# Pooled attention and a tanh MLP in one kernel: w2 in another order, its sums spread over two groups, leftover scores in one visit

## The chip, the cores and the metric

The kernel runs on one core of a Trainium2 chip. The metric is the device time of one execution in microseconds: the median over runs. The engines named below are TensorE (PE in the profile, with its weight loads as PEld), VectorE (DVE), ScalarE (ACT), GpSimd (POOL) and SyncE (SP, which here only issues transfers). They run their own instruction lists in order and wait for each other by semaphores.

## The reference

For each of 8 batches and 8 heads, q, k and v are 576 tokens by 64. k and v are averaged over runs of 8 tokens, which leaves 72 pooled tokens; every token of q attends to them. The heads are then laid side by side, which gives 4608 tokens by 512, and an MLP follows whose activation is h - tanh(h):

```python
k_p = k.reshape(B, H, Sp, pool, D).mean(axis=3)      # Sp = 576 / 8 = 72
v_p = v.reshape(B, H, Sp, pool, D).mean(axis=3)
scores = scale * np.matmul(q, k_p.transpose(0, 1, 3, 2))
attn = softmax(scores)
x = np.matmul(attn, v_p).transpose(0, 2, 1, 3).reshape(B * S, H * D)
h = x @ w_in                                         # 512 -> 2048
out = (h - np.tanh(h)) @ w_out                       # 2048 -> 512
```

Inputs and output are float32; the kernel computes the matmuls in 16-bit types and sums in float32.

## The kernel before

**Groups and batches.** The MLP works on 9 groups of 512 tokens. Group g (0 to 7) is the first 512 tokens of batch g, and group 8 gathers the last 64 tokens of all batches (`xT_last`). While TensorE works on the MLP of group g, the attention of batch g + 1 is mixed in between, one visit at a time. All instruction order is written out by hand (`tc.manual_schedule()`): the order of the calls in the source is the order on each engine.

**The MLP of groups 1 to 8.** `h_pair` makes two of the 16 hidden tiles (8 matmuls on `w1b`, line 534), ACT takes the tanh of both (line 546) and DVE subtracts (`Gt`, line 547). With `NP` = 8, pairs 0 to 6 are followed by pair 7 in two halves (`h_one`, lines 551 and 552). The second product isn't made as one 2048 by 512 matmul but in seven products of half the rows and half the columns (`products`, line 614), which are combined by a few additions. They need sums of blocks of w2, held in `w2s`, and sums of hidden tiles (`P`, `Q`, `Dg`, lines 555 to 570). With w2 as 16 tiles of 128 rows, b11 and b12 are the left and right columns of tiles 0 to 7, b21 and b22 those of tiles 8 to 15. `w2s[0]` is b11 + b22, `[1]` b11 + b12, `[2]` b21 + b22, `[3]` b21 - b11 and `[4]` -b22; b12 itself is replaced by b22 - b12. The seven products use, in order, `w2s[3]`, b11, `w2s[4]`, b12, `w2s[0]`, `w2s[1]`, `w2s[2]`, each in two halves of four tiles, so there are 14 steps u. `w_sum` (line 573) makes a sum, over a part k0 to k1 of the eight tiles.

**Group 0** runs while weights are still coming. It uses the plain product: `mlp_o` (line 517) adds four w2 tiles to one of four token blocks, in 16 steps u: `qd` = u // 4 is the set of four w2 tiles, `tb` = u % 4 the token block. Around these steps stand the attention of batch 1 and the sums of w2 that group 1 needs. w2 comes in four transfers of 512 KB (`load_w2`), issued by POOL: the first two early, the last two (`mid`) between the first and second step of pooling k of batch 1 (`pool_k(1)`, lines 256, 263, 266). SP's load of k of batch 2 is made to wait for the third w2 transfer (`after(load_k(2), w2_dmas[2])`). In the steps of group 0:

- u = 3: TensorE turns the pooled k of batch 1 (`kd`, line 320), DVE copies it to `KB`; from here also the turns of q (line 225), copied by ACT.
- u = 4: DVE makes all of `w2s[1]`, then pools v; POOL then makes `w2s[3]` in four parts, held back until v is pooled.
- u = 4 to 8: the scores of batch 1, tile by tile.
- u = 9 and 11: ACT makes `w2s[4]`.
- u = 9 to 13: `av` makes x for token blocks 0 to 3 and, as block 4, the last 64 tokens; `x_pe_transpose` (line 467) turns blocks 0 to 3, and ACT copies them to `xT` (line 474). The fourth turn stands ahead of step 14.
- u = 12 to 15: the finished token blocks are copied out of PSUM, by ACT for tb 0 and 2 and by DVE for tb 1 and 3 (line 526).

The rest of the sums is made on DVE: b12 after group 0, `w2s[0]` in four parts behind pairs 0 to 3 of group 1, and `w2s[2]` in two halves after products 1 and 2 of group 1.

**Scores.** 144 pooled tokens of two heads don't fit in 128 rows, so four tiles hold 128 rows each and the four leftovers of 16 rows are packed as tile `NM` = 4: four matmuls with 32 columns of weights each, which write four strips of one PSUM bank. `scores_wide(b, (t,))` makes 512 tokens of one tile and its Exp (line 374); `scores_tail(b)` makes the last 64 tokens of all five tiles, tiles 0 to 3 first, and their Exp (line 380). In groups 1 to 6, step u = 4 of the products is followed by the leftover tile's 512 tokens and step u = 5 by the tail.

**After the products.** DVE's `gate` instruction (line 635, after product 2) releases POOL's pooling of k and v of the batch after next. ACT's copy (line 644) and DVE's subtraction (line 645) follow product 4. `x_dma_transpose` (line 452) has SP transpose x for the next group.

Of the kernel before, what the change touches and what calls it, by code (L numbers as in the profile page):

```python
# [8 lines left out]
FP32 = mybir.dt.float32  # L9
BF16 = mybir.dt.bfloat16  # L10
F16 = mybir.dt.float16
ACT = mybir.ActivationFunctionType
ALU = mybir.AluOpType
PSUM = bass.MemoryType.PSUM

B, H, S, D = 8, 8, 576, 64
# [5 lines left out]
QA = 128 * R  # L22
QT = S - QA
# [6 lines left out]
NT = 5  # L30
# [2 lines left out]
LO = PR - 128  # L33
KP = 160
NM = 4
HT = TG // 2
HD = DM // 2
NP = NHID // 2
# [4 lines left out]
def kernel(  # L43
# [202 lines left out]
    def halves(n, b):  # L246
        return ((0, n),) if b < 2 else ((0, n // 2), (n // 2, n))

    def pool_k(b, eng, t0=0, t1=NT, mid=(), dep=None):
        r = k_raw[b % 2].rearrange("p t (j d) -> p t j d", d=D)[:, t0:t1, :, :]  # L250
        if b not in kdups:
            kdups[b] = work.tile([128, NT, 2, D], BF16, name="kd", tag="kd")
        kd = kdups[b][:, t0:t1, :, :]
        n = t1 - t0
        for ta, tb in halves(n, b):
            first = eng.tensor_tensor(  # L256
                out=r[:, ta:tb, 0:4, :], in0=r[:, ta:tb, 0:4, :], in1=r[:, ta:tb, 4:8, :], op=ALU.add
            )
            if dep is not None and ta == 0:
                after([first], dep)  # L260
        for c in mid:
            load_w2(c)
        eng.tensor_tensor(
            out=r[:, :, 0:2, :], in0=r[:, :, 0:2, :], in1=r[:, :, 2:4, :], op=ALU.add
        )
        eng.tensor_tensor(
            out=kd,
            in0=r[:, :, 0:1, :].to_broadcast([128, n, 2, D]),
            in1=r[:, :, 1:2, :].to_broadcast([128, n, 2, D]),
            op=ALU.add,  # L270
        )
        return first

    def pool_v(b, eng):
        r = v_raw[b % 2].rearrange("p t (j d) -> p t j d", d=D)
# [100 lines left out]
    def scores_tail(b):  # L376
        ps = ps_any([128, NT, QT], FP32, "s_ps")
        for t in range(NT):
            score_mms(b, t, ps[:, t, :], True)
        nc.scalar.activation(  # L380
            out=E_tiles[b][:, :, QA:S], in_=ps[:, :, :], func=ACT.Exp, scale=SCALE
        )

    def av_mms(b, blk, half, ps):
        E = E_tiles[b]
# [77 lines left out]
    def x_pe_transpose(b, blk, x_sb):  # L463
        xf = x_sb.rearrange("p a h d -> p (a h d)")
        ps = ps_any([128, NFB, 128], FP32, "xT_ps")
        for fb in range(NFB):
            nc.tensor.matmul(
                ps[:, fb, :],
                lhsT=xf[:, fb * 128 : (fb + 1) * 128],
                rhs=ident[:, :],  # L470
                start=True,
                stop=True,
            )
        nc.scalar.copy(out=xT[b % 2][:, blk, :, :], in_=ps[:, :, :])
# [33 lines left out]

    o_tiles = {}

    def mlp_o(g, tb, i0, i1, gts, pool=None):
        if i0 == 0:
            p, tag = pool or (ps_o, "o_ps")
            o_tiles[tb] = p.tile([128, DM], FP32, name="o_ps", tag=tag)
        o_ps = o_tiles[tb]
        for i in range(i0, i1):
            nc.tensor.matmul(  # L517
                o_ps[:, :],
                lhsT=gts[i][:, tb * 128 : (tb + 1) * 128],
                rhs=w2b[:, i, :],  # L520
                start=(i == 0),
                stop=(i == NHID - 1),
            )
        if i1 == NHID:
            o_sb = O[:, tb, :]
            (nc.vector.tensor_copy if g == 0 and tb % 2 else nc.scalar.copy)(
                out=o_sb, in_=o_ps[:, :]
            )
            nc.sync.dma_start(out=out_part(g, tb, tb + 1), in_=O[:, tb : tb + 1, :])

    def h_mms(g, i, dst):
# [40 lines left out]
    def w_sum(out, a, b, op, eng=nc.vector, k0=0, k1=NP):  # L572
        return eng.tensor_tensor(  # L573
            out=out[:, k0:k1, :], in0=a[:, k0:k1, :], in1=b[:, k0:k1, :], op=op
        )
# [90 lines left out]
        )  # L666

    def load_w2(c):
        w2_dmas.append(
            nc.gpsimd.dma_start(  # L670
                out=w2b[:, c * 4 : (c + 1) * 4, :], in_=w2_src[:, c * 4 : (c + 1) * 4, :]
            )
        )

    def after(lds, dep):
# [205 lines left out]
    for i in range(5, NHID):  # L881
# [5 lines left out]
        if i == 11:  # L887
            av(0, 4, ps_any, False)
            x_dma_transpose(0, 2)
    pool_k(1, nc.gpsimd, mid=(2, 3))  # L890
    after(load_k(2), w2_dmas[2])
    load_v(2)
    o_pools = [(ps_o, "o_ps"), (ps_o, "o_ps"), (ps_h, "hT_ps"), (ps_h, "hT_ps")]
    pend = []
    for u in range(16):
        qd, tb = u // 4, u % 4
        if u == 14:
            x_pe_transpose(1, *pend.pop(0))
        mlp_o(0, tb, qd * 4, qd * 4 + 4, gts, o_pools[tb])
        if u == 0:  # L900
            q_cast(1, nc.scalar.copy, 2)
            load_q(2)
        if u == 3:
            k_transpose(1, ps_any, (nc.vector.tensor_copy, nc.vector.tensor_copy))
            q_pe_transpose(1, (0,), "act")
        if u == 4:
            q_pe_transpose(1, (1,), "act")
            w_sum(w2s[:, 1, :, :], b11, b12, ALU.add)
            v1_done = pool_v(1, nc.vector)
            after(  # L910
                [
                    w_sum(w2s[:, 3, :, :], b21, b11, ALU.subtract, nc.gpsimd, k, k + 2)
                    for k in range(0, NP, 2)
                ],
                v1_done,
            )
        if u in (5, 6):
            q_pe_transpose(1, (u - 3,), "act")
        if 4 <= u <= 8:
            scores_wide(1, (u - 4,))  # L920
        if u == 6:
            q_pe_tail(1)
        if u == 8:
            scores_tail(1)
        if u in (9, 11):
            n = (u - 9) // 2
            nc.scalar.mul(
                out=w2s[:, 4, 4 * n : 4 * n + 4, :], in_=b22[:, 4 * n : 4 * n + 4, :], mul=-1.0
            )
        if u >= 9:  # L930
            if 11 <= u <= 13:
                x_pe_transpose(1, *pend.pop(0))
            if u <= 13:
                x_sb = av(1, u - 9, ps_any, False)
                if u < 13:
                    pend.append((u - 9, x_sb))
    pool_k(2, nc.gpsimd)
    pool_v(2, nc.gpsimd)
    w_sum(b12, b22, b12, ALU.subtract)
# [1 line left out]
    for g in range(1, NG):  # L941
        nb = g + 1 if g + 1 < B else None
        nn = g + 2 if g + 2 < B else None
        for p in range(NP - 1):
            c = p if g > 1 else p - 1
            if nb is not None and 0 <= c < 3:
                q_cast_part(nb, c)
            h_pair(g, p, ((2, 0, 4, 6, 0, 2, 4) if g == 1 else (0, 2, 4, 6, 0, 2, 4))[p], p % 2)
            if g == 1 and p < 4:
                w_sum(w2s[:, 0, :, :], b11, b22, ALU.add, k0=2 * p, k1=2 * p + 2)  # L950
            if 3 <= p < 6:
                sum_p(2 * p - 6, 2 * p - 4)
            if nb is not None and p == 0:
                k_dma_transpose(nb)
            if g == 1 and p == 0:
                x_dma_transpose(1, 2)
            if g > 1 and p == 0:
                store(g - 1, 2, 4, nc.gpsimd)
                store(g - 1, 0, 2, nc.gpsimd)
            if nb is not None and p == 0:  # L960
                k_place(nb, nc.gpsimd.tensor_copy)
            if nb is not None and 0 <= c < 3:
                q_dma_transpose(nb, c)
            if nb is not None and c == 2:
                if nn is not None:
                    load_k(nn)
                    load_v(nn)
                    load_q(nn)
        h_one(g, NP - 1, 1, 0, 2)
        h_one(g, NP - 1, 0, 1, 3)  # L970
        sum_p(6, 8)
        sum_q(0, 4)
        sum_q(4, 8)
        ps_a = Banks(2, 3, 4, 5, 0, 1)
        for u in range(14):
            n, half = u // 2, u % 2
            bk, lhs, rhs = products[n]
            if n == 6 and g == NG - 1:
                break
            product(g, bk, lhs, rhs, 4 * half, 4 * half + 4, n < 2)  # L980
            if half:
                after_product(g, n)
                if g == 1 and n in (1, 2):
                    w_sum(w2s[:, 2, :, :], b21, b22, ALU.add, k0=4 * n - 4, k1=4 * n)
            if nb is not None:
                if u < NT:
                    scores_wide(nb, (u,))
                if u == NT:
                    scores_tail(nb)
                if u in (5, 6, 7, 8, 10):  # L990
                    blk = (5, 6, 7, 8, 10).index(u)
                    av(nb, blk, ps_b1, True)
                    if blk in (1, 3, 4):
                        x_dma_transpose(nb, blk // 2)
                if u == 6 and nn is not None:
                    pool_k(nn, nc.gpsimd, dep=gate[0])
                    pool_v(nn, nc.gpsimd)
        if g < NG - 1:
            nc.scalar.copy(out=O[:, 0:2, 0:HD], in_=chain(g, C1))
# [37 lines left out]
```

## Time and profile before

| | us |
|---|---|
| median of 3 runs | 291.96 (291.9 to 292.7) |
| the profiled execution | 292.5 |
| its span | 290.8 |
| granted TensorE clock (mean) | 0.998 |
| TensorE busy | 280.6 |
| DVE busy | 220.1 |
| ACT busy | 151.1 |
| POOL busy | 118.7 |

The span is what the profile's rows cover; all times of rows are counted from its start. A row of a timeline has its start, its duration, the engine, the line of the source, the operation, what it writes and reads, how many instructions it joins, and in brackets how long the engine was idle before it and what ended that. Matmuls overlap: a 128x512 one lasts 0.379 in the rows, but the next starts 0.216 later, so for TensorE the distance between starts counts. `128*32` is the shape of the weights: 128 rows, 32 columns. The chain of waits is the list of work that ended last, followed back from the end.

### The profile page before, as it was taken

The page shows a single profiled execution, that of the slowest core. Times are in us where ns is not written, and L with a number is a line of the kernel's source. Part 1 is how long each engine was busy: PE and PEld are TensorE (multiplying, and loading weights), DVE is VectorE, ACT ScalarE, POOL GpSimd, SP SyncE. Part 2 cuts the span into 40 slices and gives each one's busy share as a digit, 9 for nine tenths or more (in the row PEclk, how much of TensorE's full clock was granted, in tenths as well). Part 3 has the DMA queues.
Part 4 walks back from the last instruction along what each step waited for, and adds up shares of the span by engine and source line. Part 5 has one row for each costly group of instructions (what it writes and reads, how often), then busy time and mean ns, then how long its engine had stood idle before and what let it go on. Part 6 is the DMA issues. An engine that isn't in the chain of part 4 may idle for free.

```text
span 290.8 us, 5231 instructions
## 1 busy us (share of the span) xinstructions
PE 280.6 (96%) x2031; PEld 177.7 (61%) x2032; DVE 220.1 (76%) x349; ACT 151.1 (52%) x216; POOL 118.7 (41%) x128
## 2 busy tenths in 40 slices
PE   7899989998999999999999999999999999999994
PEld 3454445544874589447944795479547954884583
DVE  6558757799984998499839993999389938945983
ACT  4737476585527660866086608661766146315510
POOL 8600726993099109910992089208930010010000
PEclk9999999999999999999999999999999999999999
DMA  7999999998745994599458956895560340012014
GB/s 249 225 213 277 301 156 299 322 199 299 190 80 108 303 315 91 111 283 344 82 108 262 352 97 106 252 352 108 100 163 0 62 166 2 1 52 95 0 36 111
DMA packets 64104, 49.95 MB, mean 172 GB/s; under 512 B 39248, under 2 KB 53072, under 8 KB 64080
## 3 DMA queue, kind: packets, MB, share of 16 engines
q1 hardware_dynamic: 54592, 35.60, 46.8%
q0 software_dynamic: 6768, 12.06, 19.0%
q10 hardware_dynamic: 2720, 1.97, 2.4%
q8 instruction: 16, 0.26, 0.4%
q14 instruction: 8, 0.07, 0.1%
HBM read 36.70 MB, written 9.44 MB: 159 GB/s over the span
## 4 chain that ended last, share of the span: by engine, by line
PE 75%; DMA 9%; DVE 6%; POOL 4%; ACT 2%; issue 1%; SPq 0%; POOLq 0%; DVEq 0%; ACTq 0%
PE PS L534 34%; PE PS L590 30%; DMA w1b<-in_moe_w_in_dram 5%; DMA k_raw<-in_k_dram 4%; PE PS L391 4%; PE PS L517 4%; PE PS L359 3%; DVE Gt L547 2%; DMA xT<-x_sb 1%; POOL k_raw L256 1%; DVE w2s L573 1%; DVE P L555 1%; ACT TS L546 1%; DVE x_sb L424 1%; ACT q_bf L193 1%
## 5 line engine op out<-in xcount | busy, mean ns | idle before, releaser
L534 PE MATMUL PS<-xT,w1b 128*128 128x512 bf16 x448 | 98.0, 379 | 1.2 <-DMA xT<-x_sb 0.7
L547 DVE TENSOR_TENSOR Gt<-PS,TS 128x1024 bf16<-128x1024 f32 x56 | 68.3, 1220 | 37.6 <-ACT TS L546 37.6
L534 PEld LDWEIGHTS <-w1b 128*128 128x128 f16 x512 | 49.9, 98 | 60.6 <-issue 1.9
L546 ACT ACTIVATE TS<-PS 128x1024 f32<-128x1024 f32 x56 | 57.3, 1024 | 31.6 <-PE PS L534 27.4
L256 POOL TENSOR_TENSOR k_raw<-k_raw 128x512 f32<-128x512 f32 (+2 forms) x13 | 21.1, 1639 | 83.3 <-DVE rden L423 53.8
L590 PE MATMUL PS<-w2s,Dg 128*128 128x256 f16 x256 | 30.2, 273 | 0.0
L374 ACT ACTIVATE E<-PS 128x512 bf16<-128x512 f32 x40 | 23.7, 598 | 12.0 <-PE PS L359 11.9
L590 PEld LDWEIGHTS <-P 128*128 128x128 bf16 x256 | 24.5, 98 | 6.1 <-issue 1.4
L590 PEld LDWEIGHTS <-Gt 128*128 128x128 bf16 x256 | 24.2, 98 | 6.1 <-DVE Gt L552 0.5
L606 POOL DMA_DIRECT2D out_dram<-O x14 | 7.8, 557 | 46.4 <-DVE O L647 44.2
L590 PEld LDWEIGHTS <-Dg 128*128 128x128 bf16 x256 | 24.8, 98 | 2.8
L555 DVE TENSOR_TENSOR P<-Gt 128x1024 bf16<-128x1024 bf16 x32 | 22.4, 699 | 0.5
L644 ACT COPY m<-PS 128x512 f32<-128x512 f32 x8 | 4.7, 585 | 31.8 <-PE PS L590 31.8
L391 PE MATMUL PS<-VB,E 128*128 128x130 bf16 x240 | 20.2, 220 | 0.1
L565 DVE TENSOR_TENSOR Dg<-Gt 128x1024 bf16<-128x1024 bf16 x32 | 19.9, 683 | 0.0
L277 POOL TENSOR_TENSOR v_raw<-v_raw 128x512 f32<-128x512 f32 (+1 forms) x12 | 19.4, 1640 | 0.0
L391 PEld LDWEIGHTS <-E 128*128 128x128 bf16 x240 | 16.3, 98 | 2.0 <-issue 0.4
L424 DVE TENSOR_TENSOR x_sb<-PS,rden 128x512 bf16<-128x512 f32 x24 | 16.6, 691 | 0.8
L590 PE MATMUL PS<-w2s,Gt 128*128 128x256 f16 x128 | 16.7, 273 | 0.4 <-DVE Gt L552 0.2
L590 PE MATMUL PS<-w2s,P 128*128 128x256 f16 x128 | 16.3, 273 | 0.0
L590 PE MATMUL PS<-w2s,Q 128*128 128x256 f16 x128 | 16.3, 273 | 0.0
L590 PE MATMUL PS<-w2b,P 128*128 128x256 f16 x128 | 16.3, 273 | 0.0
(114 smaller groups left out, 388.0 us busy)
## 6 DMA issues: line engine op xcount, KB each, us to landing
k_raw<-in_k_dram SPq DMA_DIRECT2D x7, 1024.0 KB, 7.7
q_raw<-in_q_dram SPq DMA_DIRECT2D x7, 1024.0 KB, 12.4
v_raw<-in_v_dram SPq DMA_DIRECT2D x7, 1024.0 KB, 11.4
out_dram<-O POOLq DMA_DIRECT2D x14, 512.0 KB, 4.6
w1b<-in_moe_w_in_dram POOLq DMA_DIRECT2D x4, 512.0 KB, 14.5
w2b<-in_moe_w_out_dram POOLq DMA_DIRECT2D x4, 512.0 KB, 18.6
out_dram<-O SPq DMA_DIRECT2D x4, 256.0 KB, 5.6
k_raw<-in_k_dram SPq DMA_DIRECT2D x7, 128.0 KB, 8.3
```

The source lines that it names most:

```text
L256: first = eng.tensor_tensor(out=r[:, ta:tb, 0:4, :], in0=r[:, ta:tb, 0:4, :], in1=r[:, ta:tb, 4:8, :], op=ALU.add)
L277: eng.tensor_tensor(out=r[:, ta:tb, 0:4, :], in0=r[:, ta:tb, 0:4, :], in1=r[:, ta:tb, 4:8, :], op=ALU.add)
L374: nc.scalar.activation(out=E[:, t, 0:QA], in_=ps[:, :], func=ACT.Exp, scale=SCALE)
L391: nc.tensor.matmul(ps[:, 2 * n : 2 * n + 2, :].rearrange("p h d -> p (h d)") if n < 2 else ps.rearrange("p (a s) d -> p a s d", s=2)[:, :, ...
L424: nc.vector.tensor_tensor(out=x_sb[:, :, :, :], in0=ps[:, :, :, 0:D], in1=rden[:, :, :, :].to_broadcast([128, 2, 4, D]), op=ALU.mult,)
L517: nc.tensor.matmul(o_ps[:, :], lhsT=gts[i][:, tb * 128 : (tb + 1) * 128], rhs=w2b[:, i, :], start=(i == 0), stop=(i == NHID - 1),)
L534: nc.tensor.matmul(dst, lhsT=w1b[:, fb, i * 128 : (i + 1) * 128], rhs=x[:, :, fb, :], start=(fb == 0), stop=(fb == NFB - 1),)
L546: nc.scalar.activation(out=t2, in_=PS[:, b0 : b0 + 2, :], func=ACT.Tanh)
L547: nc.vector.tensor_sub(out=Gt[:, p, :, :], in0=PS[:, b0 : b0 + 2, :], in1=t2)
L555: nc.vector.tensor_tensor(out=P[:, a:b, :], in0=Gt[:, a:b, 0, :], in1=Gt[:, a:b, 1, :], op=ALU.add)
L565: return nc.vector.tensor_tensor(out=Dg[:, a:b, :, :], in0=Gt[:, a:b, :, 0:HT], in1=Gt[:, a:b, :, HT:TG], op=ALU.subtract,)
L590: nc.tensor.matmul(part(g, bk, tt), lhsT=lhs(k, slice(tt * 128, (tt + 1) * 128)), rhs=rhs[:, k, :], start=(first and k == 0 and (tt == 0 o ...
```

## The change

- The four transfers of w2 bring tiles 0 to 3, 8 to 11, 4 to 7 and 12 to 15 (`W2_ORDER`), and group 0 uses them in this order.
- The last step of pooling k of batch 1 (`kd`) is made by DVE instead of POOL. POOL's first two parts of `w2s[3]` (tiles 0 to 3) follow that step; its other two still wait until v is pooled.
- At u = 4, DVE makes the first halves (k 0 to 3) of `w2s[1]`, `w2s[0]` and `w2s[2]` ahead of pooling v, and the second half of `w2s[1]` behind it. In group 1 only the second halves of `w2s[0]` (two parts, behind pairs 0 and 1) and of `w2s[2]` (after product 4, behind line 645) are left.
- `scores_ends` replaces the leftover tile's visit and the tail's visit, in group 0 at u = 8 and in groups 1 to 6 at u = 4: the leftover tile's 512 tokens, its 64 tail tokens, the tail of tiles 0 to 3, and then both Exp.
- In group 0, `av` of batch 1's last tokens comes after step 15, and the fourth turn of x after step 14 instead of ahead of it.
- All four token blocks of group 0 are copied out by ACT.

```diff
+W2_ORDER = (0, 8, 4, 12)
-    def pool_k(b, eng, t0=0, t1=NT, mid=(), dep=None):
+    def pool_k(b, eng, t0=0, t1=NT, mid=(), dep=None, last=None):
...
-        eng.tensor_tensor(
+        kd_done = (last or eng).tensor_tensor(
             out=kd,
...
-        return first
+        return kd_done
...
+    def scores_ends(b):
+        E = E_tiles[b]
+        ps = ps_any([128, QA], FP32, "s_ps")
+        pt = ps_any([128, NT, QT], FP32, "s_ps")
+        score_mms(b, NM, ps[:, :], False)
+        for t in (NM, 0, 1, 2, 3):
+            score_mms(b, t, pt[:, t, :], True)
+        nc.scalar.activation(out=E[:, NM, 0:QA], in_=ps[:, :], func=ACT.Exp, scale=SCALE)
+        nc.scalar.activation(out=E[:, :, QA:S], in_=pt[:, :, :], func=ACT.Exp, scale=SCALE)
...
-    def mlp_o(g, tb, i0, i1, gts, pool=None):
-        if i0 == 0:
+    def mlp_o(g, tb, qd, gts, pool=None):
+        if qd == 0:
...
-        for i in range(i0, i1):
+        i0 = W2_ORDER[qd]
+        for i in range(i0, i0 + 4):
...
-        if i1 == NHID:
-            o_sb = O[:, tb, :]
-            (nc.vector.tensor_copy if g == 0 and tb % 2 else nc.scalar.copy)(
-                out=o_sb, in_=o_ps[:, :]
-            )
+        if qd == 3:
+            nc.scalar.copy(out=O[:, tb, :], in_=o_ps[:, :])
...
     def load_w2(c):
+        i = W2_ORDER[c]
...
-                out=w2b[:, c * 4 : (c + 1) * 4, :], in_=w2_src[:, c * 4 : (c + 1) * 4, :]
-            )
+            nc.gpsimd.dma_start(out=w2b[:, i : i + 4, :], in_=w2_src[:, i : i + 4, :])
...
-    pool_k(1, nc.gpsimd, mid=(2, 3))
+    kd1 = pool_k(1, nc.gpsimd, mid=(2, 3), last=nc.vector)
+    after([w_sum(w2s[:, 3, :, :], b21, b11, ALU.subtract, nc.gpsimd, k, k + 2) for k in (0, 2)], kd1)
...
     for u in range(16):
         qd, tb = u // 4, u % 4
-        if u == 14:
-            x_pe_transpose(1, *pend.pop(0))
-        mlp_o(0, tb, qd * 4, qd * 4 + 4, gts, o_pools[tb])
+        mlp_o(0, tb, qd, gts, o_pools[tb])
...
         if u == 4:
             q_pe_transpose(1, (1,), "act")
-            w_sum(w2s[:, 1, :, :], b11, b12, ALU.add)
+            w_sum(w2s[:, 1, :, :], b11, b12, ALU.add, k1=4)
+            w_sum(w2s[:, 0, :, :], b11, b22, ALU.add, k1=4)
+            w_sum(w2s[:, 2, :, :], b21, b22, ALU.add, k1=4)
             v1_done = pool_v(1, nc.vector)
             after(
                 [
                     w_sum(w2s[:, 3, :, :], b21, b11, ALU.subtract, nc.gpsimd, k, k + 2)
-                    for k in range(0, NP, 2)
+                    for k in (4, 6)
                 ],
                 v1_done,
             )
+            w_sum(w2s[:, 1, :, :], b11, b12, ALU.add, k0=4)
...
-        if 4 <= u <= 8:
+        if 4 <= u <= 7:
             scores_wide(1, (u - 4,))
...
         if u == 8:
-            scores_tail(1)
+            scores_ends(1)
...
-        if u >= 9:
-            if 11 <= u <= 13:
-                x_pe_transpose(1, *pend.pop(0))
-            if u <= 13:
-                x_sb = av(1, u - 9, ps_any, False)
-                if u < 13:
-                    pend.append((u - 9, x_sb))
+        if 11 <= u <= 14:
+            x_pe_transpose(1, *pend.pop(0))
+        if 9 <= u <= 12:
+            pend.append((u - 9, av(1, u - 9, ps_any, False)))
+        if u == 15:
+            av(1, 4, ps_any, False)
...
-            if g == 1 and p < 4:
-                w_sum(w2s[:, 0, :, :], b11, b22, ALU.add, k0=2 * p, k1=2 * p + 2)
+            if g == 1 and p < 2:
+                w_sum(w2s[:, 0, :, :], b11, b22, ALU.add, k0=2 * p + 4, k1=2 * p + 6)
...
-                if g == 1 and n in (1, 2):
-                    w_sum(w2s[:, 2, :, :], b21, b22, ALU.add, k0=4 * n - 4, k1=4 * n)
+                if g == 1 and n == 4:
+                    w_sum(w2s[:, 2, :, :], b21, b22, ALU.add, k0=4)
             if nb is not None:
-                if u < NT:
+                if u < NM:
                     scores_wide(nb, (u,))
-                if u == NT:
-                    scores_tail(nb)
+                if u == NM:
+                    scores_ends(nb)
```

More of the change, by code (lines that the diff above doesn't have):

```diff
@@ L668, in load_w2 @@
     def load_w2(c):
+        i = W2_ORDER[c]
         w2_dmas.append(
-            nc.gpsimd.dma_start(
-                out=w2b[:, c * 4 : (c + 1) * 4, :], in_=w2_src[:, c * 4 : (c + 1) * 4, :]
-            )
+            nc.gpsimd.dma_start(out=w2b[:, i : i + 4, :], in_=w2_src[:, i : i + 4, :])
         )
```

## The prediction

> **What bounds the kernel now.** I read the page, then the granted clock, then the busy time by stretch, the chain of waits, and last the timelines of the engines in the stretches that the change touches.
>
> ```profile
> span 290.8 us, 5231 instructions
> PE 280.6 (96%) x2031; PEld 177.7 (61%) x2032; DVE 220.1 (76%) x349; ACT 151.1 (52%) x216; POOL 118.7 (41%) x128
> ```
>
> By stretch (length, then busy time of PE, PEld, DVE, ACT, POOL, the granted clock and DMA):
>
> ```profile
> 55.24:69.71 14.47, 13.98 (x66) 6.27 (x65) 13.53 (x15) 9.33 (x10) 12.07 (x11) 1.00 0.97 243
> 69.71:86.90 17.19, 16.13 (x159) 13.16 (x158) 16.17 (x28) 6.70 (x13) 7.10 (x5) 1.00 0.66 172
> 116.51:146.02 29.51, 29.51 (x223) 19.61 (x223) 23.02 (x34) 16.09 (x22) 15.50 (x16) 1.00 0.76 202
> ```
>
> TensorE bounds it, at a granted clock of 1.00. Group 3 (116.51 to 146.02) is 29.51 us of TensorE without a gap; group 1 (55.24 to 86.90) takes 31.66, and in it DVE is busy 29.70 of 31.66. So the question is group 1's DVE, and what TensorE does in the other groups. The chain of waits shows where DVE leads:
>
> ```profile
> 63.65 1.14 DVE Gt L547
> 64.79 0.98 DVE w2s L573
> 65.77 1.02 DVE P L555
> ...
> 71.52 0.61 DVE Gt L552
> 72.17 0.39 PE PS L590 x2
> ...
> 83.72 3.04 DMA xT<-x_sb
> ```
>
> From 63.65 DVE never rests until the last half of Gt; the first product's last two matmuls start only at 72.17, and the next group waits for the transposed x until 86.90 (0.67 idle). TensorE's own timeline around the moved parts:
>
> ```profile
> 38.56 0.45 PE L320 MATMUL PS<-ident,kd 128*128 128x128 bf16 x5 [0.86 <-POOL kd L266]
> 44.35 1.02 PE L517 MATMUL PS<-w2b,Gt 128*128 128x512 f16 x4
> 53.29 0.38 PE L467 MATMUL PS<-ident,x_sb 128*128 128x128 bf16 x4 [0.32 <-ACT xT L474]
> 135.55 0.40 PE L359 MATMUL PS<-qT,KB 128*32 128x512 bf16 x4
> 135.88 1.05 PE L590 MATMUL PS<-w2s,P 128*128 128x256 f16 x8
> 136.77 0.42 PE L359 MATMUL PS<-qt,KB 128*128 128x64 bf16 x8
> 137.12 0.52 PE L391 MATMUL PS<-VB,E 128*128 128x130 bf16 x6
> ```
>
> The numbers to take are the distances between starts.
>
> **kd of batch 1 on DVE: 0.** POOL's last step (1.54) goes; DVE does it in 0.82, the 128x640 f32 add at 43.56. TensorE would start the turn at 37.85, not 38.56. But the first score then waits for ACT's copy of qT: ACT casts q without a gap from 37.07 (its DMA) to 39.5 and ends that copy at 40.06, so the score starts at 40.1 instead of 40.20. And at 44.35 the third set of w2 tiles in the output product waits for the third w2 transfer: TensorE was free at 44.22, and SP's load of k, held by the same transfer, issues at 44.32. Its place among POOL's issues (33.80) is the same. So of 0.7 nothing remains; bounds 0 and 0.1. The three half sums put ahead of v's pooling on DVE (3 x 0.60 from about 39.3, blocked by POOL's two sums until 40.3 at worst) end by 42.1; v's transfer lets pooling start at 42.03. The fourth (0.69 behind it, done 46.7) precedes the first reciprocal, which comes at 47.0. POOL's other two sums now wait for the last w2 transfer (ACT waited for it until 47.95) and end at 50.25; POOL's next work waits for k until 51.00 in either kernel.
>
> **Leftover scores in one visit: 0.20 a visit, seven visits.** In group 3 the product ahead of the narrow (128*32) matmuls takes 0.97 to them (134.58 to 135.55), elsewhere 0.87: 0.10 in. Out of them 0.33 for a stream that costs 0.22 at full width: 0.11 out. The tail's four full and four narrow ones take 0.35; a stream of 64 columns is an eighth of 0.22, 0.03, and if the narrow four run side by side as the wide four do, that is 5 x 0.03, so here too 0.2 is going in and out. The new order (NM wide, NM tail, then 0 to 3) goes in and out once: 0.20 saved. No row shows a narrow matmul behind another on the same strip; if it drained in between, 0 is saved, and if strip after strip drained, it costs 0.1 x 3 = 0.3 extra. I take 0.20, the row nearest by being the same instructions. The tail's Exp (0.44) now stands ahead of ACT's copy L634: E ends 136.6, the Exp 136.95, and the product that L634 waits for now ends 137.1, so DVE's chain behind it, up to the x that the next group waits for, is at most 0.1 later. The transposed x lands 0.4 to 0.7 ahead of its use in groups 3 to 6 (in group 4 issued at 171.7, 3.1 to land, used at 175.46) and about 0.3 in group 2, which covers this and the 0.20. The Trainium skill, "TensorEngine Tiling (Array Packing)", Key Properties, says that a change of tiling mode, and not of the tile alone, drains the engine; by it 0.20 stands and both bad ends fall, and no run here shows it yet.
>
> **Batch 1's last tokens behind group 0: 0.55.** At 53.29 the fourth x turn sits in the bank of the third, 0.48 after av's last matmul could have handed over; in the new order the turn takes a bank read long before, and av (0.35) fills the end while ACT copies the last xT (done 54.3). The third av loses its 0.07 delay too. All four O copies are ACT's: the last ends at 54.9, its bank is wanted at 56.2, and the first Tanh comes at 56.4. With 0.20 for the visit, group 1 starts at 54.5 instead of 55.24: -0.75. The last tokens' reciprocals end at 55.6 and then the b12 sum starts; before it waited for the O copy until 56.05.
>
> **Group 1, first part.** The tanh chain moves by 0.75, so Gt of pair 3 starts at 62.9. The sum at 64.79 (0.98 on the chain) is gone. From there 8.4 us remained to 72.05; now 7.4, ending at 70.3 (-1.75). But DVE and POOL hold each other up, as rows of the two engines' timelines show:
>
> ```profile
> 64.45 1.05 POOL L291 TENSOR_TENSOR VB<-v_raw,mask 128x512 bf16<-128x512 f32 x1
> 64.70 1.07 DVE L573 TENSOR_TENSOR w2s<-w2b 128x512 f16<-128x512 f16 x1
> ...
> 79.64 3.04 POOL L256 TENSOR_TENSOR k_raw<-k_raw 128x512 f32<-128x512 f32 x2 [11.96 <-DVE m L635]
> 82.76 1.54 POOL L263 TENSOR_TENSOR k_raw<-k_raw 128x640 f32<-128x640 f32 x1
> 83.61 1.23 DVE L645 TENSOR_TENSOR m<-m,m 128x512 f32<-128x512 f32 x1
> 84.37 1.87 POOL L266 TENSOR_TENSOR kd<-k_raw 128x640 bf16<-128x640 f32 x1
> ```
>
> The same sum took 0.41 elsewhere; here it ended when L291 had. One more such block (0.66) gives -1.1. I take the middle, -1.4: 72.17 becomes 70.77.
>
> **Group 1, products.** From 72.17 to the last product's end (83.45 + 24 x 0.109 = 86.07) are 13.90; less 0.20, 13.70: TensorE could be done at 84.47. DVE loses two sums of 0.60, so L635 ends at 77.15 and the last x at 81.05; its transpose (3.1) lands at 84.15 and the 0.67 goes. What is late next is the sum left behind L645. POOL starts 0.15 after L635 (as 138.46 after 138.32): 77.3, then 3.05, 1.54 and kd. L645 can start at 81.4 (product 4 plus 0.2 and ACT's copy of 0.58), waits for POOL's L263 until 82.0 as it did at 83.61, ends 82.5; kd (1.40 when alone) takes its turn to 83.9; the sum follows, 0.60, to 84.5. TensorE, done with product 4 at 82.23 less 1.60, wants it four visits later, at 80.6 + 0.87 + 0.35 + 0.87 + 0.87 = 83.55: it waits 0.95. If DVE keeps its turn, the sum ends at 83.1 and nothing waits. I take 0.95, by the alternation at 64.45. The Trainium skill, "SBUF — State Buffer", Who interferes with whom, says the same against this change: a two-input DVE operation and a reading GpSimd one exclude each other, the first to issue keeping the port; with the rule the sum has the 0.95, without it -3.5 instead of -2.5. Queued behind the late sum on DVE are the last tokens' x and L647, wanted by pair 3 of group 2 at the earliest. Group 2 then starts at 85.4, not 86.90: **-1.5**. The bounds: with -1.1 and a wait of 1.2, -0.9; with -1.75 and none, -2.8.
>
> **Groups 2 to 6:** five visits, -1.0 (bounds 0 and -1.2). **Sum: -2.5.** The profiled execution took 292.5 for its span of 290.8, 0.54 over the median; it would become 290.0, and the median 291.96 becomes **289.5**.
>
> **Rivals.**
> - *The late sum does not wait.* For it: L645 itself got its turn between two POOL operations. Against: it waited for the one ahead. Sum -3.5, 288.5.
> - *One visit saves nothing*, a drain lying between the narrow matmuls. For it: no row has two on one strip. All seven 0.20 go: -1.1, 290.9.
> - *Slower:* the narrow tail drains strip by strip, +0.3 a visit instead of -0.2. Against: the four wide ones run at once (0.40 for four). Sum -1.1 + 7 x 0.3 = +1.0, 293.0; it decides from 0.16 a visit.
> - *The change is hidden:* group 1 stays bound by DVE because POOL's moved operations block it more. The DVE it loses is 2.5 us of rows; two blocks more in each half (4 x 0.66) eat it. Then -0.75 - 1.0 + 1.3, 291.5.
>
> **Numbers.** Forecast 0.50 (own range 288.9 to 290.2), late sum not waiting 0.20, one visit worth nothing 0.16, hidden 0.06, slower 0.08. The low end takes in the second with 0.3 more, 288.2; the high end the third, 291.0. What a measurement of this kernel can tell is 0.3%, 0.88 us: faster means under 291.1. The third case lies at that edge, so 0.04 of it counts as same, with the hidden one: faster 0.82, same 0.10, slower 0.08.
>
> **What would show it.** In the profile after: the turn of kd without the 0.86, the output product still at 44.3; one 12-matmul visit, 0.5 to the next product; group 1 from 54.5; no wait for xT at group 2; a wait of TensorE for the w2s sum near 83.5; groups of 29.2 to 29.3. Wrong if group 3's length does not shrink, or if group 2 starts after 86.

## The result, and the profile after

The changed kernel took 290.9 us (median of 4 runs, 290.51 to 291.36) against 292.07 for the kernel before: ratio 0.9957, 95% interval 0.9935 to 0.9978, or 1.2 us (0.6 to 1.9) faster. Timed again in five rounds it gave 0.9945 (0.9924 to 0.9966), 1.6 us. The forecast was 289.5, 2.5 us faster. The sign was right, the time lies inside the stated range, and the gain was about half of the forecast.

The profiled execution took 290.51 for a span of 288.8, 2.0 us below the profiled execution of before. Its page, and the same stretches as before (length, then busy time of PE, PEld, DVE, ACT, POOL, the granted clock and DMA):

```profile
span 288.8 us, 5227 instructions
...
PE 279.3 (97%) x2032; PEld 176.7 (61%) x2032; DVE 223.5 (77%) x348; ACT 152.0 (53%) x218; POOL 116.9 (40%) x127
```

```profile
44.39:54.58 10.19, 10.19 (x90) 5.95 (x90) 6.65 (x21) 7.21 (x13) 6.81 (x5) 1.00 1.01 294
54.58:85.58 31.00, 29.89 (x226) 19.33 (x223) 29.74 (x42) 15.86 (x22) 18.91 (x16) 1.00 0.86 218
85.58:115.16 29.58, 29.39 (x225) 19.43 (x223) 23.96 (x35) 16.25 (x23) 15.36 (x16) 1.00 0.80 203
115.16:144.54 29.38, 29.38 (x223) 19.43 (x223) 23.46 (x34) 15.93 (x22) 15.33 (x16) 1.00 0.77 203
144.54:173.76 29.22, 29.22 (x223) 19.48 (x224) 23.44 (x34) 16.09 (x22) 15.38 (x16) 1.00 0.74 204
```

In the second view, the first line is the end of group 0, from the third set of w2 tiles to the first matmul of group 1: 10.19, where it was 10.89 (44.35 to 55.24). Group 1 takes 31.00 instead of 31.66. Groups 2 and 3 still take 29.58 and 29.38; only from group 4 on is a group 29.22, 0.22 below its 29.44. TensorE's timeline:

```profile
37.28 0.44 PE L321 MATMUL PS<-ident,kd 128*128 128x128 bf16 x5
38.07 0.40 PE L226 MATMUL PS<-ident,q_bf 128*128 128x128 bf16 x4 [0.35 <-ACT q_bf L185]
...
40.02 0.38 PE L360 MATMUL PS<-qT,KB 128*128 128x512 bf16 x1 [0.46 <-ACT qT L133]
...
44.39 1.02 PE L529 MATMUL PS<-w2b,Gt 128*128 128x512 f16 x4 [0.20 <-DMA w2b<-in_moe_w_out_dram]
45.34 0.40 PE L360 MATMUL PS<-qT,KB 128*32 128x512 bf16 x4
45.57 0.42 PE L360 MATMUL PS<-qt,KB 128*32 128x64 bf16 x8
45.83 1.03 PE L529 MATMUL PS<-w2b,Gt 128*128 128x512 f16 x4
...
53.15 0.39 PE L478 MATMUL PS<-ident,x_sb 128*128 128x128 bf16 x4
...
54.23 0.51 PE L402 MATMUL PS<-VB,E 128*128 128x130 bf16 x6
...
70.91 0.39 PE L599 MATMUL PS<-w2s,Gt 128*128 128x256 f16 x2 [0.20 <-DVE Gt L561]
...
84.71 1.03 PE L599 MATMUL PS<-w2s,Dg 128*128 128x256 f16 x8 [0.83 <-DVE w2s L582]
...
115.16 1.02 PE L543 MATMUL PS<-xT,w1b 128*128 128x512 bf16 x4 [0.20 <-DMA xT<-x_sb]
```

The wait for kd is gone and its time is lost again in three other waits: for ACT's cast of q, for its copy of qT, and for the w2 transfer. The visit takes 0.49 from 45.34 to 45.83. The fourth turn of x (53.15) waits for nothing, and the last tokens follow (54.23). The late sum is waited for, 0.83, and group 3 waits for the transposed x. The prediction named all of these but the wait for the cast and the last one; what else it missed shows on ACT:

```profile
56.57 1.02 ACT L555 ACTIVATE TS<-PS 128x1024 f32<-128x1024 f32 x1 [1.55 <-PE PS L543]
58.22 1.04 ACT L194 CAST q_bf<-q_raw 128x1024 bf16<-128x1024 f32 x1 [0.63 <-DMA q_raw<-in_q_dram]
59.17 1.02 ACT L555 ACTIVATE TS<-PS 128x1024 f32<-128x1024 f32 x1
```

Group 1's first Tanh came 0.66 earlier than before (57.23). Then ACT's cast of batch 2's q waited for its transfer, and the second Tanh began at 59.17, where in the kernel before it began at 59.19. The chain of waits of this profile runs through that transfer (start, duration, what):

```profile
48.12 10.02 DMA q_raw<-in_q_dram
58.22 0.68 ACT q_bf L194
59.17 1.02 ACT TS L555
...
63.50 1.23 DVE Gt L556
...
82.63 2.03 DVE w2s L582
84.71 1.03 PE PS L599 x8
```

The Gt at 63.50 is that of pair 3, which the prediction had at 62.9; before, it was at 63.57.

### The profile page after: what moved, and what is told of

The parts are those of the page before. It is cut to its first block, busy times and chain, and to the rows that moved or that the text cites. A ratio compares the mean times of both kernels' runs of the same rounds, so it can differ in the third digit from the quotient of the medians.

```text
span 288.8 us, 5227 instructions
## 1 busy us (share of the span) xinstructions
PE 279.3 (97%) x2032; PEld 176.7 (61%) x2032; DVE 223.5 (77%) x348; ACT 152.0 (53%) x218; POOL 116.9 (40%) x127
## 4 chain that ended last, share of the span: by engine, by line
PE 69%; DMA 17%; DVE 6%; POOL 3%; ACT 2%; issue 2%; SPq 1%; POOLq 0%; DVEq 0%; ACTq 0%
PE PS L543 34%; PE PS L599 29%; DMA w1b<-in_moe_w_in_dram 4%; DMA w2b<-in_moe_w_out_dram 4%; DMA k_raw<-in_k_dram 4%; DMA q_raw<-in_q_dram 3%; PE PS L402 3%; PE PS L360 3%; DVE Gt L556 2%; DMA xT<-x_sb 1%; POOL k_raw L257 1%; ACT TS L555 1%; DVE x_sb L435 1%; DVE P L564 1%; DVE w2s L582 1%
## 5 line engine op out<-in xcount | busy, mean ns | idle before, releaser
L543 PEld LDWEIGHTS <-w1b 128*128 128x128 f16 x512 | 49.9, 98 | 59.5 <-issue 1.0
L375 ACT ACTIVATE E<-PS 128x512 bf16<-128x512 f32 x33 | 19.5, 598 | 7.7 <-PE PS L360 7.6
L402 PEld LDWEIGHTS <-E 128*128 128x128 bf16 x240 | 16.9, 98 | 2.1 <-issue 0.4
L1008 ACT COPY O<-PS 128x512 f32<-128x512 f32 x7 | 4.1, 586 | 23.4 <-PE PS L599 23.4
L599 PE MATMUL PS<-w2b,Gt 128*128 128x256 f16 x128 | 16.3, 273 | 0.0
```

The source lines that it names most:

```text
L375: nc.scalar.activation(out=E[:, t, 0:QA], in_=ps[:, :], func=ACT.Exp, scale=SCALE)
L402: nc.tensor.matmul(ps[:, 2 * n : 2 * n + 2, :].rearrange("p h d -> p (h d)") if n < 2 else ps.rearrange("p (a s) d -> p a s d", s=2)[:, :, ...
L543: nc.tensor.matmul(dst, lhsT=w1b[:, fb, i * 128 : (i + 1) * 128], rhs=x[:, :, fb, :], start=(fb == 0), stop=(fb == NFB - 1),)
L599: nc.tensor.matmul(part(g, bk, tt), lhsT=lhs(k, slice(tt * 128, (tt + 1) * 128)), rhs=rhs[:, k, :], start=(first and k == 0 and (tt == 0 o ...
```

## The experiments

Line numbers move by 1 to 12 against the kernel before. Since the start of the third w2 set differs from execution to execution (43.4 to 44.4 us in these profiles, with no visible tie to the kernel), I compare stretches that start there. Each row is one profiled execution; its ratio is that of the medians, against runs of the kernel before in the same session:

| profile | third w2 set to group 1 | group 1 | groups 2 to 6 | ACT's wait for q | ratio to before (95%) |
|---|---|---|---|---|---|
| before | 10.89 | 31.66 | 147.27 | none | 1 |
| after | 10.19 | 31.00 | 146.62 | 0.63 | 0.9957 (0.9935 to 0.9978) |
| changed again | 10.20 | 31.86 | 146.92 | 1.40 | 0.9945 (0.9924 to 0.9966) |
| visit alone | 10.68 | 31.73 | 146.76 | none | 0.9977 (0.9961 to 0.9993) |
| two visits | 10.41 | 30.53 | 147.41 | 0.48 | 0.9954 (0.9936 to 0.9973) |
| kd on POOL | 10.19 | 31.80 | 146.77 | 0.8 | 0.9952 (0.9934 to 0.997) |
| sums early | 10.20 | 31.61 | 146.61 | 2.43 | 0.9894 (0.9862 to 0.9926) |
| q later | 10.19 | 31.00 | 146.88 | none | 0.9919 (0.9898 to 0.9941) |
| sums early, q later | 10.19 | 29.78 | 146.84 | none | 0.9883 (0.9864 to 0.9902) |
| the same, one Dg first | 10.19 | 29.99 | 146.42 | none | 0.9869 (0.9841 to 0.9896) |
| one Dg first | 10.20 | 31.87 | 146.50 | 1.1 | 0.9934 (0.991 to 0.9958) |
| before, q later | 10.90 | 32.02 | 147.23 | 0.43 | 0.999 (0.997 to 1.001) |
| x first | 10.20 | 35.48 | 157.24 | 1.35 | 1.0444 (1.042 to 1.0469) |
| sums early, q later, x first | 10.19 | 33.22 | 158.91 | 0.83 | 1.0424 (1.0401 to 1.0448) |

**The changed kernel again.**

> The changed kernel once more, timed in five rounds and profiled again. Theory A (the terms hold, the size of the first measurement is the spread of single executions): the profiles of before and after differ by 2.0 us of span, so the ratio should come out near 0.993, 2.0 us below before. Theory B (the leftover visit's gain of 0.22 in each of groups 2 to 6 is eaten by the wait for the transposed x, which landed only just in time in the first profile): near 0.996, 1.2 us, and the new profile shows waits of TensorE for xT at the starts of three or more of groups 2 to 7, together 0.5 us or more.

The ratio, 0.9945, lies between the two theories. The profile explains the gap between profiles and medians: the first pair of profiles flattered the change. Here group 1 takes 31.86, more than before, and groups 2, 3 and 5 lose 0.32, 0.24 and 0.26 of the visit's gain (29.54, 29.46 and 29.48 instead of 29.22), 0.8 in all, as theory B has it. As a named wait only 0.2 of it shows, but the place is the same in all three: the last 24 product matmuls take 2.94, 2.86 and 2.88 to the first matmul on the new xT, and 2.62 where a group is clean. TensorE's row in group 1, and the ACT rows behind it:

```profile
61.55 7.19 PE L543 MATMUL PS<-xT,w1b 128*128 128x512 bf16 x32 [0.62 <-DVE Gt L556]
```

```profile
55.86 1.02 ACT L555 ACTIVATE TS<-PS 128x1024 f32<-128x1024 f32 x1 [1.55 <-PE PS L543]
58.28 1.05 ACT L194 CAST q_bf<-q_raw 128x1024 bf16<-128x1024 f32 x1 [1.40 <-DMA q_raw<-in_q_dram]
59.23 1.02 ACT L555 ACTIVATE TS<-PS 128x1024 f32<-128x1024 f32 x1
```

Group 1 started at 53.87, but q landed at 58.2, as in the first profile. The first Tanh is 0.71 earlier than in the first profile, the second is 0.06 later. Pair 4 needs the bank of pair 1, so it waits for pair 1's Gt, and the 0.6 is TensorE's.

**The visit alone, and the change without it.**

```diff
# visit alone: the kernel before, with scores_ends
-        if 4 <= u <= 8:
+        if 4 <= u <= 7:
             scores_wide(1, (u - 4,))
...
-            scores_tail(1)
+            scores_ends(1)
...
-                if u < NT:
+                if u < NM:
                     scores_wide(nb, (u,))
-                if u == NT:
-                    scores_tail(nb)
+                if u == NM:
+                    scores_ends(nb)
# two visits: the changed kernel, with these lines the other way round
```

> The kernel before with the one visit for the leftover scores and nothing else. Theory A: 0.2 at group 0 and 0.22 in each of groups 2 to 6, 1.3 us in all (group 1's own visit is hidden by DVE): ratio 0.9955. Theory B: the wait for xT takes back what exceeds the slack of each group; in the profile before, that slack was 0.1 to 0.4 in group 2 and 0.3 to 0.7 later, so 0.6 to 0.9 us are left: ratio 0.997 to 0.998. A visit that saved nothing would give 1.000.

> The changed kernel with the leftover tile and the tail in two visits again; all else as changed. Both theories: groups 2 to 6 as long as before (29.44 us), the start of group 2 at 85.8 instead of 86.90; span 1.1 us below before, ratio 0.996. If the first measurement's 1.2 us were the sums and the last tokens alone, this run equals the changed kernel; by theory A it is 1.1 us slower than the changed kernel, by theory B 0.5 us or less.

Alone the visit is worth 0.0023, 0.7 us (0.2 to 1.1): theory B's size, not the 1.3 of the terms. Group 0's part is 0.21 (10.89 to 10.68) and three of the five groups take 29.22; group 2 takes 29.57 and group 5 29.53, and at the start of group 2 the wait for xT of the kernel before (0.67) is longer:

```profile
86.33 4.04 PE L544 MATMUL PS<-xT,w1b 128*128 128x512 bf16 x18 [0.81 <-DMA xT<-x_sb]
```

Without the visit the change gives 0.9954, 0.3 us slower than with it (0.9945), which is the same within the intervals: theory B's side, not theory A's 1.1. Group 1 took 30.53 there; in that execution q held ACT up by 0.48 only and the late sum TensorE by 0.5. Groups 3 to 6 took 29.44 each again.

**kd on POOL again.**

```diff
-    kd1 = pool_k(1, nc.gpsimd, mid=(2, 3), last=nc.vector)
+    kd1 = pool_k(1, nc.gpsimd, mid=(2, 3))
```

> The changed kernel with the last step of pooling k of batch 1 on POOL again. Prediction's step (kd on DVE is worth nothing, since the third w2 transfer is awaited at 44.3 either way): ratio as the changed kernel, within 0.001; TensorE's wait for kd (0.9 us) is back and the third set of w2 tiles starts when its transfer lands all the same. Rival (the wait for kd was worth its 0.7 us): 0.002 slower.

0.9952 against 0.9945 and 0.9957: worth nothing that can be measured. The third set started at 43.42. The wait for kd did not come back, though: in that execution k landed early enough for POOL, so its profile shows the step only for such an execution.

**The sums early.**

```diff
             pend.append((u - 9, av(1, u - 9, ps_any, False)))
+        if u == 12:
+            w_sum(w2s[:, 0, :, :], b11, b22, ALU.add, k0=4)
+            w_sum(w2s[:, 2, :, :], b21, b22, ALU.add, k0=4)
...
-            if g == 1 and p < 2:
-                w_sum(w2s[:, 0, :, :], b11, b22, ALU.add, k0=2 * p + 4, k1=2 * p + 6)
...
-                if g == 1 and n == 4:
-                    w_sum(w2s[:, 2, :, :], b21, b22, ALU.add, k0=4)
```

> The changed kernel with the upper halves of the first and third sum of w2 also made by DVE in group 0, in the 2.2 us in which it had nothing to do before the last tokens; group 1 makes no sums of these any more. If the late sum behind line 645 is what costs 0.83 us, TensorE's wait in product 6 is gone and group 2 starts 0.8 to 1.0 us earlier, at 84.6 to 84.8: ratio 0.003 below the changed kernel's. Rival: the transposed x is late next (it was issued at 81.35 and needs 3.1), so that 0.5 us or less is won. A second rival: POOL's pooling of batch 2, which shares the time with the moved sums, is late and takes it back: nothing won.

The ratio fell by 0.005, more than the 0.003 expected, and the wait in product 6 is gone. But in the profiled execution, which at 290.49 was 0.8 above the run's median, group 2 started only at 85.54, because a new wait took the place of the old one. TensorE's and ACT's rows:

```profile
62.66 7.07 PE L543 MATMUL PS<-xT,w1b 128*128 128x512 bf16 x32 [1.65 <-DVE Gt L556]
```

```profile
59.38 1.04 ACT L194 CAST q_bf<-q_raw 128x1024 bf16<-128x1024 f32 x1 [2.43 <-DMA q_raw<-in_q_dram]
```

q landed at 59.4 there, and TensorE waited 1.65 for a Gt that was late for it. None of my three answers had this wait; it names the cause that the next runs test.

**q later.** The casts of batch 2's q go behind pairs 1, 2 and 3 of group 1.

```diff
-            c = p if g > 1 else p - 1
+            c = p if g > 1 else p - 2
```

> The changed kernel with ACT's three casts of batch 2's q one pair later in group 1 (behind pairs 1, 2 and 3 instead of 0, 1 and 2). Theory C (the step that failed is 'the tanh chain moves by 0.75': q of batch 2 lands at 58.2 whenever group 1 starts, and the first cast, waiting for it, holds the second Tanh back): ACT's wait of 0.6 to 1.4 us for q is gone, the third and fourth Gt start 0.5 us or more after group 1's start earlier than in the changed kernel, TensorE's wait for Gt in group 1 (0.6 us in the second profile) is gone, group 1 from 31.0 to 31.9 down to 30.5 or less; ratio 0.002 to 0.003 below the changed kernel's 0.9945. Rival D (group 1 is bound by DVE and POOL blocking each other, whenever Tanh comes): group 1 stays at 31 us or more, ratio as the changed kernel.

> Upper halves of two sums in group 0's idle DVE time, and the q casts one pair later. With the sums early alone, TensorE's 0.83 for the late sum went but TensorE waited 1.7 us for Gt, behind a q that landed at 59.4. Theory C: that 1.7 goes too, group 1 takes 29.8 to 30.3 us (31.6 with the sums early alone); ratio 0.986 to 0.988. Rival D: 31 us or more, ratio 0.9894 as without the later casts.

> The kernel before with only the q casts one pair later in group 1. Theory C: q had landed when ACT came to it in the kernel before, so nothing is won: ratio 0.999 to 1.001. If the casts' place were a gain of its own (the second Tanh no longer behind a cast of 1.04 us), 0.997.

ACT's rows of the changed kernel with q later:

```profile
55.66 1.02 ACT L555 ACTIVATE TS<-PS 128x1024 f32<-128x1024 f32 x1 [1.55 <-PE PS L543]
57.38 1.02 ACT L555 ACTIVATE TS<-PS 128x1024 f32<-128x1024 f32 x1 [0.70 <-PE PS L543]
58.30 1.04 ACT L194 CAST q_bf<-q_raw 128x1024 bf16<-128x1024 f32 x1
```

The second Tanh now follows TensorE, not q: it starts 3.71 after group 1, where the two profiles of the changed kernel have 4.59 and 5.36. The third Gt starts 6.79 after group 1 instead of 7.54 and 8.76; in the kernel before it was 6.86, so the chain now moves with group 1. The wait for Gt at pair 4 is gone. The ratio is 0.0026 lower, as theory C had it, though the two intervals overlap. Group 1, at 31.00, missed the 30.5 and is where rival D had it: the late sum still costs 0.8, and POOL's turns cost DVE more (the b12 sum took 2.29, and 1.60 and 1.22 in two profiles of the changed kernel). With the sums early as well, nothing of this is left, and group 1 falls from 31.61 to 29.78, in theory C's range.

These are single executions, though, and the 31.61 is of one with a late q (59.4). By the medians the later casts are worth 0.0026 alone and 0.0011 on top of the early sums (0.9883 for 0.9894), neither clear of the noise. The early sums are worth 0.0051 alone and 0.0036 on top of the later casts, with intervals that barely touch. So the rows show that q holds the Tanh chain of the changed kernel, and D alone can't be all of it; the price of q, 0.3 to 0.8 us by these medians, is not settled.

In the kernel before, the same edit gives 0.999 (0.997 to 1.001). That q had landed in time there holds for the profile of before and for "visit alone"; in this run's own, q landed at 59.5, ACT waited 0.43 for it even in the later place, and group 1 took 32.02. That DVE's sums bound group 1 there, whatever q does, fits this but is not shown.

**x earlier.**

```diff
# x first: the second half of the Dg sums behind the fourth x
-    def after_product(g, n):
+    def after_product(g, n, dk=NP):
...
-            for k in range(0, NP, 2):
+            for k in range(0, dk, 2):
                 sum_d(k, k + 2)
...
-                after_product(g, n)
+                after_product(g, n, NP if nb is None else 4)
...
                     av(nb, blk, ps_b1, True)
+                    if blk == 3:
+                        sum_d(4, 6)
+                        sum_d(6, 8)
# one Dg first: only the first sum, into DVE's idle 0.38 us
+            sum_d(0, 2)
             nc.vector.tensor_tensor(out=O[:, 2:4, 0:HD], in0=chain(g, C2), in1=m4, op=ALU.add)
-            for k in range(0, NP, 2):
+            for k in range(2, NP, 2):
```

> The same, and in groups 1 to 6 the second half of the Dg sums is made behind the fourth x instead of ahead of the first, so that x is turned up to 1.2 us earlier. Theory B (the one visit's gain is partly eaten by the wait for xT): no wait for xT at the start of groups 2 to 7, groups 2 to 6 at 29.22 us each; 0.3 to 0.8 us below the kernel without this, ratio 0.984 to 0.986. Rival: the later Dg sums reach product 5 too late, and TensorE waits there for DVE instead: groups 29.3 to 29.5 us.

> The changed kernel with only the Dg sums in the new place. Theory B: groups 2 to 6 sum to 146.1 us (146.6 to 146.9 in the two profiles of the changed kernel), ratio 0.001 to 0.003 below the changed kernel's 0.9945. Rival (the waits for xT are the product of two disturbed executions): no difference. In group 1 the late sum stands behind the moved sums too and may come 0.5 us later.

Both were 4% slower (1.0424 and 1.0444). That is the first expectation's rival, far beyond its size; the second had no answer for it. Rows of DVE, POOL and TensorE in group 2 of the changed kernel with x first:

```profile
115.09 3.40 DVE L574 TENSOR_TENSOR Dg<-Gt 128x1024 bf16<-128x1024 bf16 x2
```

```profile
114.47 1.53 POOL L264 TENSOR_TENSOR k_raw<-k_raw 128x640 f32<-128x640 f32 x1
116.08 1.86 POOL L267 TENSOR_TENSOR kd<-k_raw 128x640 bf16<-128x640 f32 x1
```

```profile
116.61 0.61 PE L599 MATMUL PS<-w2s,Dg 128*128 128x256 f16 x4 [0.64 <-DVE Dg L574]
118.55 1.70 PE L599 MATMUL PS<-w2s,Dg 128*128 128x256 f16 x14 [1.33 <-DVE Dg L574]
```

Two sums that take 1.28 ahead of the first x take 3.40 between POOL's operations, each waiting for one of them, and against the first profile of the changed kernel TensorE loses 4.5 us in group 1 (35.48 for 31.00), 2.0 to 3.9 in each of groups 2 to 5 and 0.2 in group 6. In group 4, the one of 3.9, the granted clock was also down to 0.95 and TensorE busy 1.5 us longer, so that part is not the sums'. This place is bad; whether the aim is right it doesn't show, so the last pair moves one sum to a time when POOL is idle.

> The changed kernel with only that one Dg sum moved. Theory B: groups 2 to 6 sum to 146.1 to 146.3 us, against 146.6 and 146.9 in the two profiles of the changed kernel; ratio 0.001 to 0.002 below it. Rival: no difference.

> All sums early and q later, and the first of the four Dg sums ahead of line 639 instead of behind it, in groups 1 to 8: DVE stood idle there for 0.38 us, waiting for ACT, and POOL is idle too. The x of the next group then comes 0.38 us earlier. Theory B (the rest of the one visit's gain is held up by xT): TensorE's waits of 0.1 to 0.36 us for xT at the starts of groups go, groups 2 to 6 take 29.2 to 29.3 us each, ratio 0.986 to 0.987 against 0.9883 without this. Rival: x is not what the groups wait for, ratio 0.988 again.

On the changed kernel groups 2 to 6 sum to 146.50, short of the 146.1 to 146.3 expected, and the ratio is 0.9934; on top of the other two edits they sum to 146.42, ratio 0.9869 instead of 0.9883. The six profiles in which these groups stand as in the changed kernel have 146.61 to 146.92, so both point to theory B; but the ratios differ by less than the intervals can separate, and in the last one groups 2 and 3 still lose 0.2 and 0.1. The last kernel is the best of all: 288.53 us, ratio 0.9869 (0.9841 to 0.9896), 3.8 us below before and some 2.3 below the changed kernel.

## Why the prediction came out at half

- **kd on DVE, 0:** right. The next waits were named too: ACT's copy of qT (0.46) and then the third w2 transfer (0.20). The transfer isn't always among them: in "changed again" SP's load of k, which the same transfer releases, was issued at 43.50, and the third set followed at 43.67 right behind TensorE's own work.
- **One visit, 0.20 each:** the visit itself was right, 0.22 measured. In it 0.23 pass from the wide to the tail matmuls and 0.26 from there to the next product; a clean group falls from 29.44 to 29.22. The Trainium skill's sentence that a change of tiling mode, not of the tile alone, drains the engine ("TensorEngine Tiling (Array Packing)", Key Properties) agrees: the second set on the same strips paid no passage.
- **Last tokens, 0.55, and group 1 from 0.75 earlier:** right, 0.70 from the third w2 set on in both profiles of the changed kernel.
- **Group 1, first part:** this step failed. "The tanh chain moves by 0.75" took for granted that ACT's chain follows TensorE. In the trace of before, the first cast of q stood between the first two Tanh without a wait (58.24), but only because q had landed just then (issued at 48.76, 9.4 to land: 58.16). Its landing does not move with group 1: SP issues it behind k and v of batch 2, and k waits for the third w2 transfer. Over the 14 profiles q landed between 57.0 and 59.6, with no visible tie to the start of group 1. So an earlier group 1 met a wait for q, of 0.63 and 1.40 in the two profiles of the changed kernel. In the first the second Tanh moved by 0.02 and pair 3's Gt by 0.07 (63.50 for 63.57) instead of 0.75. The step asked whether ACT is free, and not whether the data of the instruction queued between the two Tanh would be there.
- **Its size, -1.4 at the first product:** the first profile showed -1.26 (70.91 for 72.17), close by luck: from pair 3's Gt to there 7.41 passed, the forecast's 7.4 without the block by POOL that it had half counted in, and that made up for the Tanh. Over the three profiles whose group 1 is as changed (after, changed again, kd on POOL) group 2 starts 41.19, 42.06 and 42.00 after the third w2 set, before 42.55: -1.36, -0.49 and -0.55, mean -0.8 where the prediction has -1.5. How much of the missing 0.7 is q's and how much DVE's turns with POOL, the runs don't separate.
- **The late sum waits 0.95:** right, 0.83. L654 ended only after POOL's L264 (82.17), kd took its turn, and the sum took 2.02:

```profile
81.56 1.15 DVE L654 TENSOR_TENSOR m<-m,m 128x512 f32<-128x512 f32 x1 [0.23 <-ACT m L653]
82.63 2.02 DVE L582 TENSOR_TENSOR w2s<-w2b 128x1024 f16<-128x1024 f16 x1
```

```profile
80.63 1.54 POOL L264 TENSOR_TENSOR k_raw<-k_raw 128x640 f32<-128x640 f32 x1
82.24 1.87 POOL L267 TENSOR_TENSOR kd<-k_raw 128x640 bf16<-128x640 f32 x1
```

  The Trainium skill's rule against the change, that a two-input DVE operation and a reading GpSimd one shut each other out ("SBUF — State Buffer", Who interferes with whom), agrees with these rows, and the rival without the wait fell.
- **Groups 2 to 6, -1.0:** mis-sized. "Which covers this and the 0.20" was wrong: -0.65, -0.35 and -0.50 in the same three profiles, and -0.5 in the mean of the six with these groups as changed. DVE's chain to the fourth x and its transpose do not get shorter with the visit, and TensorE now catches up with them in one to three of the groups. The slack was also misread: the prediction takes 116.51, 146.02 and 175.46 for the starts of groups 3 to 5, but their first matmuls stand at 116.42, 145.85 and 175.29. At the end of group 3 x was issued at 142.3 and took 3.3, so 0.2 was left and not 0.4, less than the 0.20 and 0.1 asked of it. Group 3 went from 29.43 to 29.38 only. The visit alone shows it too: 0.7 us, not 1.3.
- **The sum:** -0.8 and -0.5 make -1.3, and the two measurements 1.2 and 1.6. The profiled execution of before was also a late one: its third w2 set started at 44.35, while the twelve profiles of the experiments have 43.4 to 43.9. The prediction noted its 0.54 over the median; it changes no stretch that starts at that set.
- **Rivals:** that one visit saves nothing, and that narrow matmuls drain strip by strip, both fell. "The change is hidden" named the right place, group 1's first part, and one of its holders, POOL; q's transfer it did not name, and its +1.3 is not worked out from the blocks that it counts.

Open stays why q lands between 57.0 and 59.6 and why the third w2 transfer releases SP's load of k between 42.7 and 44.4, and how much of what groups 2 to 6 lose the transposes' own landing times make.

## What to carry to other kernels

When a stage is to start earlier, list for every instruction queued in its in-order chain when its data lands, also for those that show no wait: a zero wait just behind a landing is a bound, not slack. When work is moved on DVE, look at what POOL does in the new place: the same two sums cost 1.3 us or 3.4. And compare more than one profiled execution of each kernel before a difference of 1 us is read as a term; here two executions of one kernel differed by 0.9 in a single group.

## What the runs showed of the hardware

- Narrow (32-column) matmuls behind others on the same strips pay no passage (0.23 from four streams of 512 side by side to the next set); going in and out of them costs 0.10 and 0.11 us.
- Two-input operations of DVE and POOL take turns one by one: 0.64 us each alone, 1.7 each in turn with POOL's of 1.5 and 1.9, and the price reached TensorE in five groups (14 us of span, 303.1 for 288.8, some 1.5 of it in a group with the granted clock at 0.95).
